# The prefetch hint in TensorE's tail names the loop's back edge instead of a stub's branch

## Chip, cores, metric

One core of one Trainium2 chip. The metric is the device time of one execution in microseconds (us). Executions agree within some 0.5 us, and a single execution of a kernel on one core is called "one run".

## The reference, cut to what matters

```python
def reference(A_x, A_k_cache, A_v_cache, A_wq, A_wo, B_x, B_w1, B_w2, B_w3, B_w4):
    # _A_ref: attention of one token over a cache of 65,536 places, 4 key/value heads
    # _B_ref: x1 = x + shifted(gelu(layernorm(x) @ w1)) @ w2;  x1 + gelu(layernorm(x1) @ w3) @ w4
    x = A_x
    xn = _layernorm(x, axis=-1)
    return x + _A_ref(xn, A_k_cache, A_v_cache, A_wq, A_wo) + _B_ref(xn, B_w1, B_w2, B_w3, B_w4)
```

Almost all of the time is the reading of the two caches (128 MiB) and of the weights: 169.87 MB in all, on a queue that keeps the sixteen DMA engines busy for 98.8% of the span.

## The kernel before

Operations are recorded per engine and emitted at the end. VectorE, ScalarE, GpSimd and SyncE run straight through; TensorE's attention part is a loop over the four heads. After the loop come the residual, the product with wo, and the product with w4, which arrives in four parts. By TensorE's sequencer is meant here what fetches its instructions. The profile shows the fetches as packets of 16,384 bytes on the queue q8, of the kind "instruction", four within the span of before. A prefetch hint is an instruction of its own (BRANCH_PREFETCH_HINT in the trace, 40 ns in before) that names a branch of the program. Around that last product the kernel before puts a stub: a hint that names a branch which is never reached (the one marked below), because the branch ahead of it always jumps over it.

```python
        def hinted_tail(eng, q, at, name):
            e = eng.engine
            one = eng.alloc_register(name + "_r")
            eng.reg_mov(one, 1)
            nc.br(name + "_b", engines=[e])
            label(name + "_b")
            hint = eng.mark_branch_hint_location()       # the hint stands here
            q.emit(eng, q.ops[at:])                      # the products with w4
            eng.br_eq(one, 1, on_true=name + "_end", on_false=name + "_t")
            label(name + "_t")
            eng.nop(nofuse=True)
            eng.br_eq(one, 0, on_true=name + "_b", on_false=name + "_end").branch_hint(hint)   # hinted, never run
            label(name + "_end")
        ...
        q_pe.emit(nc.tensor, q_pe.ops[:marks[0]])
        for s_, v in entry.items():
            nc.tensor.wait_ge(s_, v)
        with nc.tensor.Fori(0, HKV):
            for waits, o in zip(steps, work[0]):
                for s_, v in waits.items():
                    nc.tensor.wait_ge(s_, v)
                q_pe.emit(nc.tensor, [o])
            for s_, v in totals.items():
                nc.tensor.wait_ge(s_, v).then_inc(s_, -v)
        q_pe.emit(nc.tensor, q_pe.ops[marks[-1]:pe_cut])
        hinted_tail(nc.tensor, q_pe, pe_cut, "pe")
```

## Time and profile before

| | |
|---|---|
| time, median (range) | 400.37 us (400.35 to 400.45), 3 runs |
| span in the profile | 399.0 us |
| share of the data queue q1 | 98.8% of 16 DMA engines' span |
| busiest engine | VectorE, 55% |
| last landing of w4 | 396.47 us |

How to read it: here the DMA row is at 9 of 10 in 38 of its 40 slices and no engine is above 55%, so the stream of data sets the time, and the end of the kernel hangs on the last landing: 396.47 us, with 2.5 us from there to the end. The instruction queues q8 and q14 carry 0.07 and 0.02 MB, yet they use the same sixteen engines: of the sixteen landings of a load the last is 0.29 us behind the median ahead of q8's first packet, and 1.88 us on the load during which it came. The lines of the profile are in the prediction below.

### The profile page before, as it was taken

Reading aid. Unit: us, or ns where it says so; the run is one execution under the profiler, and the core shown is the slowest. Engines: PE = TensorE matmul, PEld = TensorE weight load, DVE = VectorE, ACT = ScalarE, POOL = GpSimd, SP = SyncE. Lnnn points to the kernel's source line nnn. Section 1 sums busy time; section 2 is a strip of 40 time slices with the busy share of each in tenths; the row PEclk is TensorE's granted clock in tenths of the full one; section 3 lists DMA queues with packets and bytes.
Section 4 is the critical chain, followed back from the end, with each engine's and each line's share of the span. In section 5 each row is a group of like instructions: output and inputs, shape, how many; then the busy total and the mean of one; then the engine's idle time right before and its main releaser. Section 6 shows DMA issues by size and latency. Waiting matters only on the chain.

```text
span 399.0 us, 3448 instructions
## 1 busy us (share of the span) xinstructions
PE 176.1 (44%) x1539; PEld 58.8 (15%) x1484; DVE 221.3 (55%) x260; ACT 23.9 (6%) x50; POOL 7.6 (2%) x31
## 2 busy tenths in 40 slices
PE   0034768148034713570357036413651462147394
PEld 0011334012001200120012001101120110012232
DVE  0024221995298549843984597269647952896200
ACT  1000000011001100110011002001100110011000
POOL 5000000000000000000000000000000000000000
PEclk9998656556755765565557555855585558555979
DMA  9999899999999999999999999999999999999995
GB/s 421 421 386 494 383 428 480 447 416 427 421 420 435 420 466 453 421 427 421 420 440 420 453 460 427 421 421 420 434 434 440 473 427 421 420 421 427 431 410 233
DMA packets 3759, 169.97 MB, mean 426 GB/s; under 512 B 548, under 2 KB 552, under 8 KB 808
## 3 DMA queue, kind: packets, MB, share of 16 engines
q1 hardware_dynamic: 3608, 169.87, 98.8%
q8 instruction: 4, 0.07, 0.1%
q10 hardware_dynamic: 144, 0.00, 0.0%
q14 instruction: 3, 0.02, 0.0%
HBM read 169.87 MB, written 0.00 MB: 426 GB/s over the span
## 4 chain that ended last, share of the span: by engine, by line
DMA 58%; DVE 25%; PE 13%; issue 1%; ACT 1%; SPq 1%; POOL 0%
DMA KV<-in_A_k_cache_dram 45%; DVE KV L460 18%; DMA KV<-in_B_w_dram 8%; DMA KV<-in_A_x_dram 6%; PE S_ps L411 3%; PE OT_ps L518 2%; DVE mrow L481 2%; PE M_ps L426 2%; PE S_ps L474 2%; PE S_ps L379 2%; ACT p_sb L496 1%; DVE Yall L395 1%; DVE pT_f L509 1%; PE PT_ps L505 1%; DVE pT_f L419 1%
## 5 line engine op out<-in xcount | busy, mean ns | idle before, releaser
L460 DVE STREAM_TRANSPOSE KV<-KV 128x4096 f32<-128x4096 f32 x32 | 140.3, 4421 | 43.3 <-DMA KV<-in_A_k_cache_dram 43.3
L474 PE MATMUL S_ps<-KV,Ycur 128*32 128x512 bf16 x512 | 60.7, 623 | 127.2 <-DVE KV L460 127.2
L518 PE MATMUL OT_ps<-KV,pT_f 128*32 128x512 bf16 x512 | 46.2, 500 | 1.2 <-DVE pT_f L509 1.2
L474 PEld LDWEIGHTS S_ps<-KV,Ycur 128*32 128x32 bf16 x512 | 14.3, 126 | 159.0 <-DVE KV L460 141.4
L496 ACT ACTIVATE p_sb<-S_ps,brun 128x1024 bf16<-128x1024 f32 x16 | 17.8, 1113 | 275.0 <-DVE brun L494 174.5
L509 DVE STREAM_TRANSPOSE pT_f<-PT_ps 128x512 f32<-128x512 f32 x32 | 22.5, 702 | 14.0 <-PE PT_ps L505 14.0
L481 DVE TENSOR_REDUCE mrow<-S_ps 128x1 f32<-128x1024 f32 x16 | 19.3, 1206 | 11.3 <-PE S_ps L474 11.3
L484 PE MATMUL M_ps<-Rm,Lmat 128*128 128x16 bf16 x16 | 3.1, 194 | 38.1 <-DVE Rm L482 38.1
L505 PE MATMUL PT_ps<-p_sb,permR 128*128 128x512 bf16 x32 | 18.4, 576 | 0.8
L529 DVE SCALAR_TENSOR_TENSOR O_acc<-O_acc,ff,OT_ps 128x512 f32<-128x512 f32 x12 | 9.0, 748 | 13.9 <-PE OT_ps L518 13.9
L518 PEld LDWEIGHTS OT_ps<-KV,pT_f 128*32 128x32 bf16 x512 | 12.9, 114 | 23.6 <-issue 15.5
L411 PE MATMUL S_ps<-KV 128*32 128x512 bf16 x88 | 12.6, 565 | 2.7 <-DVE KV L359 2.7
L339 DVE CAST KV<-KV 128x8 f32<-128x8 bf16 x1 | 0.2, 171 | 22.1 <-DMA KV<-in_A_x_dram 22.1
L578 PE MATMUL S_ps<-KV,o_bf 128*1 128x512 bf16 x64 | 9.4, 466 | 5.0 <-DMA KV<-in_A_wo_dram 5.0
L426 PE MATMUL M_ps<-ident_f,pT_f 64*128 64x2 f32 (+2 forms) x32 | 7.9, 372 | 2.5 <-DVE pT_f L419 2.5
L484 PEld LDWEIGHTS M_ps<-Rm,Lmat 128*128 128x128 bf16 x16 | 1.7, 104 | 49.3 <-DVE Rm L482 49.3
L582 DVE COPY pT_f<-S_ps 1x512 f32<-1x512 f32 x1 | 0.7, 679 | 14.4 <-PE S_ps L578 14.4
L426 PEld LDWEIGHTS M_ps<-ident_f,pT_f 64*128 64x128 f32 (+2 forms) x32 | 7.7, 326 | 5.0 <-DVE pT_f L419 3.4
L419 DVE COPY pT_f<-S_ps 64x512 f32<-64x512 f32 (+1 forms) x3 | 2.1, 685 | 11.3 <-PE S_ps L411 11.3
L364 PE MATMUL M_ps<-KV 8*128 8x8 bf16 x1 | 0.2, 181 | 16.0 <-DVE Dmat_f L363 16.0
L505 PEld LDWEIGHTS PT_ps<-p_sb,permR 128*128 128x128 bf16 x32 | 3.3, 103 | 26.7 <-ACT p_sb L496 14.7
L379 PE MATMUL S_ps<-KV 128*32 128x512 bf16 x64 | 6.2, 571 | 1.4 <-DVE KV L359 1.4
(88 smaller groups left out, 85.6 us busy)
## 6 DMA issues: line engine op xcount, KB each, us to landing
KV<-in_B_w_dram SPq DMA_DIRECT2D x1, 7168.0 KB, 48.2
KV<-in_B_w_dram SPq DMA_DIRECT2D x1, 4352.0 KB, 27.4
KV<-in_B_w_dram SPq DMA_DIRECT2D x2, 2048.0 KB, 28.2
KV<-in_B_w_dram SPq DMA_DIRECT2D x1, 1792.0 KB, 31.4
KV<-in_B_w_dram SPq DMA_DIRECT2D x1, 768.0 KB, 32.7
KV<-in_B_w_dram SPq DMA_DIRECT2D x1, 256.0 KB, 32.9
KV<-in_A_k_cache_dram SPq DMA_DIRECT2D x8, 46.6
KV<-in_A_v_cache_dram SPq DMA_DIRECT2D x8, 27.9
```

Source lines behind the costliest of these rows:

```text
L379: fns.append(lambda e, j=j, b=b, jj=jj: e.matmul(S_ps[32 * jj:32 * jj + 32, b, :], xn_bf[:, j:j + 1].broadcast_to([P, 32]), KV[:, 0, j * H ...
L411: fns.append(lambda e, j=j, k=k, mv=mv: e.matmul(S_ps[32 * (k % 4):32 * (k % 4) + 32, bank + k // 4, :], vec[:, j:j + 1].broadcast_to([P, ...
L426: fns.append(lambda e, b=b, nb=nb, c=c: e.matmul(M_ps[:, c0 + 16 * b + c:c0 + 16 * b + 4 * nb:4], pT_f[0:32 * nb, b, c:512:4], ident_f[0:3 ...
L460: _op(q_dve, lambda e: e.transpose(out=KV32[:, s, o:o + 4096], in_=KV32[:, s, o:o + 4096]), reads=[b_KV[s][sub]], writes=[b_KV[s][sub]], l ...
L474: fns.append(lambda e, we=we, cm=cm, mv=mv: e.matmul(S_ps[32 * cm:32 * cm + 32, n % 4, :], Ycur[:, we, :, :].rearrange("p a g -> p (a g)") ...
L481: _op(q_dve, lambda e: e.reduce_max(mrow[:, k:k + 1], S_ps[:, 2 * k:2 * k + 2, :].rearrange("p b c -> p (b c)"), axis=AX.X), reads=b_S[2 * ...
L496: _op(q_act, lambda e: e.activation(p_sb[:, :, :].rearrange("p b c -> p (b c)"), S_ps[:, 2 * k:2 * k + 2, :].rearrange("p b c -> p (b c)") ...
L505: _op(q_pe, lambda e: e.matmul(PT_ps[:, :], permR[:, :], p_sb[:, n % 2, :], start=True, stop=True), reads=[b_p[n % 2], b_const], writes=[b ...
L509: _op(q_dve, lambda e: e.transpose(out=pT_f[:, n % 2, :], in_=PT_ps[:, :]), reads=[b_PT], writes=[b_pT[n % 2]], loop=True)
L518: fns.append(lambda e, q=q, q4=q4: e.matmul(OT_ps[32 * q4:32 * q4 + 32, g % 2, :], pT_bf[:, n % 2, q, :, 1], KV[:, s, 8192 * sub + 512 * q ...
L529: _op(q_dve, lambda e: e.scalar_tensor_tensor(out=O_acc[:, 0:512], in0=O_acc[:, 0:512], scalar=ff[:, k:k + 1], in1=OT_ps[:, k, :], op0=ALU ...
L578: _grp(q_pe, [lambda e, j=j, jj=jj: e.matmul(S_ps[32 * jj:32 * jj + 1, 1, :], o_bf[:, j:j + 1], KV[:, 0, j * D + 512 * jj:j * D + 512 * (j ...
```

## The change

Its intent: the same hint with fewer instructions. It needs some branch to name; the loop's back edge exists already and is not run any more at this point, so the stub's move, its jump and its two branches can go.

```diff
-        def label(name):
-            nc.switch_bb(name, parent=None)
-
-        def hinted_tail(eng, q, at, name):
-            ... (the function shown above)
...
+        loop_br = [i for b in nc.m.functions[0].blocks for i in b.instructions if i.engine == nc.tensor.engine and "Branch" in i.opcode][-1]
         q_pe.emit(nc.tensor, q_pe.ops[marks[-1]:pe_cut])
-        hinted_tail(nc.tensor, q_pe, pe_cut, "pe")
+        bass.BassInstruction(loop_br).branch_hint(nc.tensor.mark_branch_hint_location())
+        q_pe.emit(nc.tensor, q_pe.ops[pe_cut:])
...
-        code = nc.m.functions[0].blocks[0].instructions
```

(The last line repeats an assignment made further up; without it the profile still counts 1539 matmuls and 1484 weight loads.)

## The prediction

From the recorded text (and in one place from the expectation of hint_loop_head) the passages are cut, and marked, that told of the hardware what no trace or run of this case shows, or went with that. Two figures that it uses without saying what shows them: it counts 256 instructions to a block, the piece of the program that one 16 KB packet brings. In before, TensorE had started 190, 439 and 707 instructions of the trace when the first three packets started, 249 and 268 from one to the next. And it puts some 2 us between the entry into a block and the packet of the next: in before the packets at 84.3, 120.7 and 376.8 us started 2.6, 1.7 and 2.4 us after the end of TensorE's last record ahead of them. The entry itself is not recorded, so these 2 us are an estimate, as are the 66 instructions and what is counted with them.

> **What bounds the kernel now.** I read the page of the profile first: busy shares, the row of DMA busy tenths, the DMA queues and the chain that ended last.

> ```profile
> PE 176.1 (44%) x1539; PEld 58.8 (15%) x1484; DVE 221.3 (55%) x260; ACT 23.9 (6%) x50; POOL 7.6 (2%) x31
> ...
> DMA  9999899999999999999999999999999999999995
> ...
> q1 hardware_dynamic: 3608, 169.87, 98.8%
> q8 instruction: 4, 0.07, 0.1%
> ...
> q14 instruction: 3, 0.02, 0.0%
> ...
> DMA 58%; DVE 25%; PE 13%; issue 1%; ACT 1%; SPq 1%; POOL 0%
> ```

> No engine is busy for more than 55% of the span, while the data queue q1 keeps the sixteen DMA engines busy for 98.8% of it: the kernel is one long stream of 169.87 MB. The change can matter in two ways only: by TensorE instructions in the tail, or by the traffic that fetches instructions (q8, four packets of 16 KB in 0.07 MB; q14, three of 8 KB), which shares those DMA engines. So I read next the chain of waits in the last 36 us and the timeline of TensorE from 389 us on (start, length, what).

> ```profile
> 363.55 32.92 DMA KV<-in_B_w_dram
> 396.47 0.04 issue
> 396.51 0.31 PE S_ps L566 x4
> 396.82 0.02 issue
> 396.85 0.42 DVE orow L648
> ```

> ```profile
> 390.24 0.61 PE L584 MATMUL S_ps<-pT_f,ident_f 64*1 64x256 f32 x8 [1.40 <-ACT pT_f L583]
> 390.77 2.03 PE L566 MATMUL S_ps<-KV,gh_bf 128*1 128x256 bf16 x68
> 394.00 0.93 PE L566 MATMUL S_ps<-KV,gh_bf 128*1 128x256 bf16 x28 [1.20 <-DMA KV<-in_B_w_dram]
> 395.86 0.50 PE L566 MATMUL S_ps<-KV,gh_bf 128*1 128x256 bf16 x12 [0.92 <-DMA KV<-in_B_w_dram]
> 396.51 0.28 PE L566 MATMUL S_ps<-KV,gh_bf 128*1 128x256 bf16 x4 [0.16 <-DMA KV<-in_B_w_dram]
> ```

> The last weight load, w4, comes in four parts (17, 7, 3 and 1 rows). TensorE finishes the 68 products of the first part at 392.80 and then stands still for 1.20, 0.92 and 0.16 us for the next three. The end is set by the landing of the last part at 396.47; behind it are only four matmuls, one copy of 0.42 us and the output DMA. Last, the pages of the lines of the stub:

> ```profile
> L670 PEldq MOVE  x1: 29/29/29, 390.3 to 390.3; - x1
> ...
> L673 PEldq BRANCH_PREFETCH_HINT  x1: 40/40/40, 390.3 to 390.3; - x1
> ...
> L675 PEldq COMPARE_BRANCH  x1: 246/246/246, 396.5 to 396.5; - x1
> ...
> L713 PEldq COMPARE_BRANCH  x4: 87/225/237, 140.8 to 373.0; - x4
> ```

> They give min/median/max in ns and the first and last start in us. The stub costs a move of 29 ns and a hint of 40 ns ahead of the w4 products, and a taken branch of 246 ns behind the last of them. The loop's own back edge costs 223 to 237 ns when taken and 87 ns the last time.

> [...] q8's packets are 16,384 bytes each, starting at 48.1, 84.3, 120.7 and 376.8 us. [...] a loop trip is 556 weight loads and matmuls (278 of each, from the counts of lines 474, 518, 505, 484, 543 and 535 over 4), more than two blocks, yet after the first trip (65.6 to 140.8 us) nothing is fetched on q8 until the loop is over. The loop stays resident. [...]

> [...] The trace has these sixteen landings for each load. With respect to the median engine the last of them is 0.29 us late at 26 us, but 1.88 us late on the load during which the fetch of 48.1 us came; then a second engine is 0.79 us late (the 8 KB fetch at 55.0), and the fetches at 84.3, 120.7 and 376.8 each make one more engine late. For w4's last part five engines are late by 1.18, 1.43, 1.57, 1.58 and 1.62 us. So one 16 KB fetch delays its engine by 1.2 to 1.7 us, and the load waits for the latest engine, not for the sum.

> [...] The trace has 87 ns not taken and 223 to 246 ns taken[...].

> **The change part by part.** The instruction order of the two kernels is the same on VectorE, ScalarE, GpSimd and SyncE. On TensorE:

> Removed ahead of the w4 products: the move, 29 ns; the unconditional branch to the next block left no record in the trace, so 0. The first w4 products could start up to 0.03 us earlier. They are followed by 1.20 us of waiting for a DMA: 0 on the path.

> Removed behind the last product: the branch of 246 ns at 396.52, done at 396.76, and an instruction and a second branch that were never run. VectorE's copy ends at 397.27 and the output's landing is waited for until 399.0, so TensorE was not last: 0 on the path.

> Kept: the hint, 40 ns, at the same place. Its branch is now the loop's back edge, behind it, with the loop's head as target. That is the open part. The built program of TensorE has 1,380 entries before and 1,374 after, labels included. The four q8 packets fit block boundaries if some 66 instructions precede the kernel's own (an estimate from where TensorE was at these times). Then the next boundary, 1,280, falls at entry 1,214: inside the first w4 group, after the hint at entry 1,151. A sequential prefetch should have followed there, about 391 us, with its packet some 2 us later. The trace has none. So I take it that the armed hint made the sequencer look at the hinted target instead, which is in a block already held. In the changed kernel the target is the head of the loop, also held (four trips without a fetch). I expect again no fetch.

> Moved: the loop's label on every engine is now the target of a hinted branch and is marked for alignment in the built program, where before it was the stub's label. With the estimate of 66 the head lies at 444, 68 short of a boundary; I don't expect it to move.

> Sum: 0 - 0 + 0 = 0.0 us, with at most 0.1 us from noise in where packets fall.

> **The rivals.** First: the hint of a branch that lies behind holds nothing back, and the block after the tail is fetched at about 391 us, 16 KB. For it: the absence of that packet before needs a cause, and the stub's branch lay ahead, in the very block being entered. Against its costing much: so far every fetch of TensorE made a new engine late, and a new engine has room: late by up to 1.2 us when w4's last landing is already 1.62 us behind the median. Cost 0; but if it falls on one of the five late engines (5 of 16, if the choice were free), 1.2 to 1.6 us, so 401.6 to 402.0.

> Second: the sequencer fetches the loop's head or shifts the blocks because of the alignment. The landing of a fetched block costs the same as above; a stall of TensorE would need over 1.20 us in the w4 group before it shows, or 396.5 us as its moment. A miss there of some 3 us (the 1.0 us packet and about 2 us ahead of it, my estimate) would leave 1.8 us: 402.2.

> Third: it gets faster, because a fetch that now delays w4 goes away. One candidate is the fetch at 376.8; but the code up to the hint is the same, entry for entry, and removing it would leave the other four late engines. Gain 0. The same holds for the 8 KB packet at 393.65, whose engine is only 0.43 us late.

> **The range and the chances.** No fetch, 80%: 400.3 to 400.5. A hidden fetch, 11%: the same. A fetch on a late engine, a moved loop or a stall, 7%: 401.5 to 402.5. Something that I don't see, 2%. The runs before lie between 400.35 and 400.45. I predict 400.4 us, 400.1 to 400.9 for eight in ten. Two per cent are 8 us, which nothing above reaches: within 2% 0.985, slower 0.01, faster 0.005.

> **What would show it.** Right: four q8 packets at the same times; w4's parts landing at 379.3, 389.6, 394.0, 395.8 and 396.5 us (wo's among them, first); the wait of 1.20 us ahead of the 28 products within 0.05 us; no compare-and-branch after the last matmul; a back edge of 223 to 237 ns as before. Wrong in the first step: a fifth q8 packet after 390 us, and a sixth late engine. Wrong in the second: a q8 packet inside the loop's later trips, or a gap inside the 68 products, which now issue in groups of four every 0.1 us. A time under 400.1 would mean that some landing came earlier, thus that a fetch left the late engines, for which I see no cause.

## The result and the profile after

The changed kernel takes 400.41 us (median of 6 runs, 400.31 to 400.60), the kernel before in the same rounds 400.42 us (6 runs, 400.35 to 400.58). The ratio is 1.0, 95% interval 0.9987 to 1.0013. A ratio here is the mean time of one kernel's fast runs over the mean of the other's of the same rounds, so not quite the ratio of the medians.

The page of the changed kernel, the DMA row and the queues:

```profile
DMA  9999999999999999999999999999999999999995
...
q1 hardware_dynamic: 3608, 169.87, 98.7%
q8 instruction: 5, 0.08, 0.1%
...
q14 instruction: 3, 0.02, 0.0%
```

There is one packet more on q8 than before, five in place of four. The chain of waits at the end, and TensorE's timeline from 389 us on:

```profile
363.63 32.91 DMA KV<-in_B_w_dram
396.54 0.04 issue
396.58 0.31 PE S_ps L566 x4
396.89 0.02 issue
396.92 0.42 DVE orow L648
```

```profile
389.67 0.61 PE L584 MATMUL S_ps<-pT_f,ident_f 64*1 64x256 f32 x8 [1.39 <-ACT pT_f L583]
390.21 2.03 PE L566 MATMUL S_ps<-KV,gh_bf 128*1 128x256 bf16 x68
394.07 0.93 PE L566 MATMUL S_ps<-KV,gh_bf 128*1 128x256 bf16 x28 [1.84 <-DMA KV<-in_B_w_dram]
395.93 0.50 PE L566 MATMUL S_ps<-KV,gh_bf 128*1 128x256 bf16 x12 [0.92 <-DMA KV<-in_B_w_dram]
396.58 0.28 PE L566 MATMUL S_ps<-KV,gh_bf 128*1 128x256 bf16 x4 [0.16 <-DMA KV<-in_B_w_dram]
```

The last load takes 32.91 us against 32.92; the waits ahead of the last two groups are the same to 0.01 us. TensorE reached w4 0.56 us earlier (390.21 against 390.77) and only waited longer for it, 1.84 us in place of 1.20. That head start isn't the stub's 0.03 us: the 64 products with wo took 8.76 us here against 9.39. Nor is it the change's: looked at once more, the kernel before took 8.76 us for them and the changed kernel 9.26 (again_before, again_after). The pages of the hint and of the loop's control lines:

```profile
L704 PEldq BRANCH_PREFETCH_HINT  x1: 50/50/50, 389.7 to 389.7; - x1
...
L695 PEldq COMPARE_BRANCH  x4: 76/219/252, 140.6 to 374.0; - x4
```

No compare-and-branch is left behind the last product.

The page does not say when a packet came; the trace records it. In this table are the starts, in us, of all 16 KB packets of q8 within the span; further the latest of the sixteen landings of w4's last part, how far it lies behind the median of the sixteen, and how many engines are over 1 us behind it. An engine counts as late whatever made it so, also by the 8 KB packets of q14, of which more below the last experiment. The experiments told of below stand in the table too.

| kernel (profiled run) | 16 KB instruction packets at | last landing | behind the median | late engines | span |
|---|---|---|---|---|---|
| before | 48.1, 84.3, 120.7, 376.8 | 396.47 | 1.62 | 5 | 399.0 |
| again_before | 48.1, 84.8, 123.0, 378.2 | 396.90 | 2.06 | 5 | 399.4 |
| after | 48.0, 84.2, **200.2**, 378.5, **394.0** | 396.54 | 1.56 | 6 | 399.1 |
| again_after | 48.0, 84.1, **200.2**, 378.2, **394.1** | 396.93 | 2.10 | 5 | 399.4 |
| no_hint | 48.1, 84.1, 123.1, 377.1, **394.2** | 396.42 | 1.64 | 5 | 398.9 |
| hint_loop_end | 48.1, 84.0, 120.4, 378.5, **393.6** | 396.38 | 1.48 | 6 | 398.9 |
| hint_ahead_loop | 47.9, 84.2, **197.9**, 378.6, **393.8** | 396.50 | 1.48 | 6 | 399.0 |
| loop_then_stub | 45.9, 84.5, 120.6, 378.3 | 396.49 | 1.58 | 5 | 399.0 |
| early_reset | 46.0, 84.3, 120.3, 378.6, **393.7** | 396.80 | 1.86 | 6 | 399.4 |
| stub_early | 46.1, 84.3, 120.6, 378.4 | 396.50 | 1.53 | 5 | 399.1 |
| stub_late | 45.8, 84.1, 120.6, 378.3 | 396.80 | 1.88 | 5 | 399.3 |
| hint_loop_head | 46.1, 82.0, **378.3, 384.9, 394.3** | 396.51 | 1.61 | 5 | 399.0 |
| one_block_more | **14.2**, 47.7, 86.5, 122.9, 378.2 | 396.62 | 1.73 | 6 | 399.1 |

(Bold: what differs from the kernel before.) So the time is as predicted, but the fetches are not: the third moved from 120.7 to 200.2 us, into the loop's second trip, and a fifth came at 394.0, in the tail.

### The profile page after: what moved, and what is told of

It reads as the page before. It is cut to its first block, busy times and chain, and to the rows that moved or that the text cites. A ratio compares the mean times of both kernels' runs of the same rounds, so it can differ in the third digit from the quotient of the medians.

```text
span 399.1 us, 3446 instructions
## 1 busy us (share of the span) xinstructions
PE 177.2 (44%) x1539; PEld 59.9 (15%) x1484; DVE 221.3 (55%) x260; ACT 23.9 (6%) x50; POOL 7.6 (2%) x31
## 3 DMA queue, kind: packets, MB, share of 16 engines
q1 hardware_dynamic: 3608, 169.87, 98.7%
HBM read 169.87 MB, written 0.00 MB: 426 GB/s over the span
## 4 chain that ended last, share of the span: by engine, by line
DMA 58%; DVE 25%; PE 13%; issue 1%; ACT 1%; SPq 1%; POOL 0%
DMA KV<-in_A_k_cache_dram 45%; DVE KV L460 18%; DMA KV<-in_B_w_dram 8%; DMA KV<-in_A_x_dram 6%; PE S_ps L411 3%; PE OT_ps L518 2%; DVE mrow L481 2%; PE M_ps L426 2%; PE S_ps L474 2%; PE S_ps L379 2%; ACT p_sb L496 1%; DVE Yall L395 1%; DVE pT_f L509 1%; PE PT_ps L505 1%; DVE pT_f L419 1%
## 6 DMA issues: line engine op xcount, KB each, us to landing
KV<-in_B_w_dram SPq DMA_DIRECT2D x1, 7168.0 KB, 48.1
```

## The experiments

Rivals: B, the loop's label, which the hint marks for alignment, moved the code; C, the fifth packet is made by the hint itself, which names a branch behind it; D, the moments vary by themselves; E, a hint holds back the next prefetch whichever block is entered. All eleven kernels gave a correct result.

**again_before** and **again_after**: both kernels once more, unchanged.

> The kernel before, unchanged, profiled once more. Theory A (a hint stays armed until its branch is passed, and when TensorE enters the block that holds the hinted branch, the hinted target is fetched in place of the next block; the target is already held, so nothing is fetched): again four 16 KB packets of instructions, near 48, 84, 121 and 377 us, and none after 390. Rival D (the moments vary from execution to execution): the third packet somewhere else, or a fifth one. Time 400.4 by both.

> The changed kernel, unchanged, profiled once more. Theory A: five packets, near 48, 84, 200, 378 and 394 us: the hint left armed at the end of one execution diverts the fetch of the first loop trip in the next one, so the third packet waits for the second trip. Rival D: the third packet at 121 or the fifth missing. Time 400.4, ratio within 0.1% of before, because the fifth packet goes to an engine that has room.

Measured: the packets of each kernel are where they were, within 2.3 us (table); the two that moved moved again. Rival D is out. again_after: 400.43 us (5 runs, 400.40 to 400.70), before in the same rounds 400.43 (9 runs, 400.19 to 400.73), ratio 1.0, interval 0.9987 to 1.0014. again_before was one run, 400.65 us: that is the noise that one look has.

**no_hint**: the changed kernel without the hint.

```diff
-        bass.BassInstruction(loop_br).branch_hint(nc.tensor.mark_branch_hint_location())
```

> The changed kernel without any hint. Theory A: nothing is armed, so the plain sequence: packets near 48, 84, 121, 377 and 394 us, five in all. Rival C (the hint of a branch that lies behind itself makes the fetch of 394 us, of the loop's head): four packets, none after 390. Rival B (the loop's label, marked for alignment through the hint, moved the blocks): as theory A here, third packet at 121. Time: 400.4 as long as the fifth packet finds an engine with room; 401.6 to 402.0 if it falls on a late one.

Measured: 48.1, 84.1, 123.1, 377.1, 394.2. The queues on its page:

```profile
q8 instruction: 5, 0.08, 0.1%
q14 instruction: 2, 0.02, 0.0%
```

The fifth packet comes without any hint, at 394.2 us, so it is the plain fetch of the next block, and rival C is out: the stub's hint takes it away (none after 376.8 us in before), the back edge's hint doesn't (394.0 in after). The third is back at 123. Time 400.36 us (5 runs, 400.18 to 400.61), ratio to before 1.0, interval 0.9986 to 1.0014: neither hint is worth any time. Not foreseen: q14 has two packets of 8 KB here, not three; the one that comes between 392.8 and 394.3 us in all twelve profiles with a hint does not come within this trace. A hint also marks a label of the program for alignment, which might be the cause; that is argued only, and no run here separates it.

**hint_loop_end**: the hint of the back edge at the end of each trip, just ahead of its branch.

```diff
             for s_, v in totals.items():
                 nc.tensor.wait_ge(s_, v).then_inc(s_, -v)
+            at_end = nc.tensor.mark_branch_hint_location()
...
+        bass.BassInstruction(loop_br).branch_hint(at_end)
-        bass.BassInstruction(loop_br).branch_hint(nc.tensor.mark_branch_hint_location())
```

> The hint of the loop's back edge moved from the tail to the end of each loop trip, just ahead of that branch; the loop's label is marked for alignment as in the changed kernel. Theory A: the hint is used up by its own branch a few instructions on, without a block being entered in between, so the sequence is plain: packets near 48, 84, 121, 377 and 394 us. Rival B (alignment): the third packet at 200 us as in the changed kernel. Time 400.4 by both; the back edge may become shorter than its 220 to 250 ns, hidden.

Measured: 48.1, 84.0, 120.4, 378.5, 393.6; one run, 400.14 us. The label carries the same mark as in the changed kernel, and the third packet is back in the first trip: rival B is out. The back edge did not become shorter: 223 to 242 ns when taken.

**hint_ahead_loop**: the same hint once, ahead of the loop.

```diff
+        ahead = nc.tensor.mark_branch_hint_location()
         with nc.tensor.Fori(0, HKV):
...
+        bass.BassInstruction(loop_br).branch_hint(ahead)
-        bass.BassInstruction(loop_br).branch_hint(nc.tensor.mark_branch_hint_location())
```

> The hint of the loop's back edge stands once, ahead of the loop, and none in the tail. Theory A: the first trip enters the block of the back edge with the hint armed, so the third packet moves from 121 to 200 us; the tail has no hint, so the fifth stays at 394: 48, 84, 200, 378, 394. If the 200 us of the changed kernel did not come from a hint armed in the first trip, the third packet is at 121 here. Time 400.4.

Measured: third packet at 197.9, a fifth at 393.8; one run, 400.37 us. A hint armed in the first trip is enough to move the third fetch into the second trip.

**loop_then_stub**: the kernel before with the back edge's hint put ahead of its stub.

```diff
         q_pe.emit(nc.tensor, q_pe.ops[marks[-1]:pe_cut])
+        bass.BassInstruction(loop_br).branch_hint(nc.tensor.mark_branch_hint_location())
         hinted_tail(nc.tensor, q_pe, pe_cut, "pe")
```

> Both hints in the tail, first that of the loop's back edge, then that of the stub. Theory A with one place for an armed hint: the second replaces the first, so as the kernel before: 48, 84, 121, 377, none after 390. With a place for each hint: 48, 84, 200, 378 and none after 390. Time 400.4 by both.

Measured: third at 120.6, no fifth; one run, 400.26 us. The second hint replaced the first: by these two moments there is one place.

**early_reset**: the stub's hint at the very start of TensorE's code, the back edge's in the tail.

```diff
+        hint = nc.tensor.mark_branch_hint_location()
         q_pe.emit(nc.tensor, q_pe.ops[:marks[0]])
...
         q_pe.emit(nc.tensor, q_pe.ops[marks[-1]:pe_cut])
+        bass.BassInstruction(loop_br).branch_hint(nc.tensor.mark_branch_hint_location())
         hinted_tail(nc.tensor, q_pe, pe_cut, "pe")
...
-            hint = eng.mark_branch_hint_location()
```

> The stub's hint at the very start of TensorE's code, and the loop's hint in the tail as in the changed kernel. If the changed kernel's third packet at 200 us comes from a hint left armed by the execution before, and there is one place for it, the early hint replaces it: third packet back at 121; in the tail the loop's hint replaces the stub's, so a fifth packet at 394. If nothing is carried over and the hint of the tail did it in another way, third packet at 200. With a place for each hint: 200, and none at 394. Time 400.4.

Measured: third at 120.3, a fifth at 393.7; one run, 400.68 us. The tail is that of the changed kernel as far as the hint goes, and a hint at the start, which by theory A overwrites what was left, puts the third fetch back. So the hint of one execution does reach into the next. One loophole: the stub's code is in this tail too, and its taken branch might have dropped the hint; no run has that code with the back edge's hint alone. The next two runs speak against it, for there a hint outlives taken branches.

**stub_early**: the kernel before with its hint moved to the very start.

```diff
+        hint = nc.tensor.mark_branch_hint_location()
         q_pe.emit(nc.tensor, q_pe.ops[:marks[0]])
...
-            hint = eng.mark_branch_hint_location()
```

> The kernel before with its hint moved from the tail to the very start of TensorE's code. Theory A: the hint waits for the block of its branch, the last one: 48, 84, 121, 377, none after 390, as before. Rival E (a hint only holds back the next prefetch, whichever block is entered): the packet at 48 is missing, TensorE stalls near 84 us for the block, and there is one at 394. Time 400.4 by theory A.

Measured: all four, none in the tail; one run, 400.37 us. The hint waited for 390 us, through three taken back edges of the loop, for the block of its own branch. Rival E is out.

**stub_late**: the kernel before with its hint behind the first 68 products of w4.

```diff
-            q.emit(eng, q.ops[at:])
+            n1 = next(i for i in range(at + 1, len(q.ops)) if q.ops[i][0] == 0 and i > at + 40)
+            q.emit(eng, q.ops[at:n1])
+            hint = eng.mark_branch_hint_location()
+            q.emit(eng, q.ops[n1:])
```

> The kernel before with the stub's hint behind the first 68 products of w4, so behind the entry into the last block at some 391 us. Theory A: on the first execution the fetch is already asked for; but the hint stays armed over the end, because its branch is never run, so later executions enter the block with it armed: 48, 84, 121, 377 and none after 390. If nothing is carried from one execution to the next: a fifth packet at 394. Time 400.4.

Measured: the hint ran at 392.8 us, and there is no fifth packet; one run, 400.56 us. This points the same way as early_reset, and here the hint outlived the stub's own taken branch at 396.9 us. That a hint so soon after the entry still stopped a fetch already asked for is not ruled out by this run alone.

**hint_loop_head**: the hint at the head of each trip, none in the tail.

```diff
         with nc.tensor.Fori(0, HKV):
+            at_head = nc.tensor.mark_branch_hint_location()
...
+        bass.BassInstruction(loop_br).branch_hint(at_head)
-        bass.BassInstruction(loop_br).branch_hint(nc.tensor.mark_branch_hint_location())
```

> The hint of the loop's back edge at the head of each trip[...], none in the tail. Theory A: every trip enters the block of the back edge with the hint armed, so the next block is never fetched in the loop; after the loop TensorE runs into it unprepared near 374 us: no packet at 121, one at about 375 on demand, and a stall of 2 to 4 us among the 32 small products of line 572, ahead of the wait for wo at 379.4 us, which hides it: time 400.4. If the stall runs beyond 379.4 us it comes out of the 1.2 us of slack ahead of the 28 products of w4. Rival B: no stall, packets as in the changed kernel.

Measured: no packet between 82.0 and 378.3 us. TensorE's timeline behind the loop:

```profile
373.91 0.50 PE L572 MATMUL S_ps<-ident_f,acc 128*1 128x64 f32 x10
380.72 1.23 PE L572 MATMUL S_ps<-ident_f,acc 128*1 128x64 f32 x20 [6.31 <-issue]
381.74 9.12 PE L578 MATMUL S_ps<-KV,o_bf 128*1 128x512 bf16 x64
...
392.79 2.79 PE L566 MATMUL S_ps<-KV,gh_bf 128*1 128x256 bf16 x96
395.91 0.93 PE L566 MATMUL S_ps<-KV,gh_bf 128*1 128x256 bf16 x16 [0.32 <-DMA KV<-in_B_w_dram]
```

"issue" is time in which the engine waited for nothing that the profile shows: 6.31 us in the middle of one group, around the packet of 378.3. It is the stall that theory A foresaw, well over the 2 to 4 us that I had guessed (an estimate, around the prediction's 3 us: 1.0 us for the packet and about 2 us ahead of it). It goes 1.3 us beyond 379.4, the landing of wo, and TensorE comes to w4 2.0 us later than in the kernel before (392.79 against 390.77). Of the three waits for w4 the first is gone (96 products run through), the second has shrunk from 0.92 to 0.32 us, and the third still stands: 0.15 us, inside the last line, which merges 12 and 4 products. Time 400.43 us (4 runs), before 400.48 (9 runs), ratio 0.9998, interval 0.9982 to 1.0013: even a stall of 6.31 us cost nothing here.

**one_block_more**: the kernel before with a block of useless instructions early on.

```diff
+        _grp(q_pe, [lambda e, k=k: e.matmul(M_ps[0:8, 480:488], (ident_bf[0:8, 0:8], selGT_bf[0:8, 0:8])[k % 2], ident_bf[0:8, 0:8], start=True, stop=True)
+                    for k in range(128)], reads=[b_const], writes=[b_M], partial=True)
```

> The kernel before with 128 small, useless matmuls early on, while TensorE is idle: 256 instructions, one block more, all later blocks shifted by exactly one. Theory of the late engines (the load waits for the latest engine, a 16 KB packet makes one engine late by 1.2 to 1.8 us, each on another one): five packets, the fifth between 5 and 15 us, one more late engine, time 400.4, within 0.1%. If packets cost by their sum, 16 KB of 170 MB is 0.04 us, not to be told apart; if it falls on an engine that is late already, 1.2 us or more: 401.6.

Measured: the extra work, in its place,

```profile
6.82 3.34 PE L362 MATMUL M_ps<-KV 8*8 8x8 bf16 x128
```

and five packets, the first at 14.2 us. Six engines are now over 1 us behind the median in place of five, the last by 1.73 us. Time 400.40 us (5 runs, 400.30 to 400.47), before 400.48 (9 runs), ratio 0.9997, interval 0.9983 to 1.0010. One more whole block costs nothing that could be measured. The time alone would also fit a price by bytes (0.04 us, as the expectation says); that the block went to an engine of its own is seen in the landings, not in the time.

What decides the time of a single run shows in the table: the span less the last landing is 2.5 to 2.6 us in all thirteen profiles, and the last landing follows from how far the latest engine is behind: 1.48 us with a span of 398.9 at the one end, 2.10 us with 399.4 at the other. The number of packets, four or five, does not order the spans.

What the longer spans have in common comes from two packets that no experiment was about, the 8 KB ones of q14 near 55 and 259 us. In before, the landings of the load that ends at 243.8 us have one engine 0.78 us behind the median and three over 1.5; at 263.2 us, after the second of these packets, none is near 0.78 any more and four are over 1.5, the latest 1.74. So both packets fell on one engine, and on one engine the delays add up; this is the fifth late engine beside the four of the 16 KB packets. The same step, by 0.95 to 0.98 us, is in all thirteen profiles. After it the latest engine is 1.61 to 1.82 us behind in the nine with spans of 398.9 to 399.1 us and 2.05 to 2.21 in the four of 399.3 and 399.4. That is read from the landings, which name no engine; no run changed these packets, so it is a fit and not a test.

## Why the prediction was right, and where it was not

- **The time**: right, 400.4 predicted, 400.41 measured, a change of nothing. The main line, no fetch at 80%, did not happen; what happened is the hidden fetch, given 11%, and it was the pricing of this rival that made the number right.
- **Removed ahead of w4, 0.03 us, off the path**: right. The wait ahead of the 28 products took in much more than that, 0.56 us in after and 2.0 us the other way in hint_loop_head. Its own check, that wait within 0.05 us of 1.20, failed: it was 1.84 us, through the faster group of wo. The check was too narrow, for the kernel before itself has 1.83 us in again_before.
- **Removed behind the last product, 246 ns, off the path**: right; it is gone, and 2.5 us still lie between last landing and end.
- **Kept: "I expect again no fetch"**: wrong, and this is the step that failed. From the missing packet I had concluded that an armed hint makes the sequencer look at the hinted target, whichever block is entered. The next block's fetch is held back only when the block of the hinted branch is entered (stub_early: the hint ran at the very start, all four packets came, and none in the tail; hint_ahead_loop: the packets at 47.9 and 84.2 us came, the third only at 197.9). Both signs that the prediction had set for this, a fifth packet after 390 us and a sixth late engine, came. Its first rival, given at most 18%, had the right ground for it: the stub's branch lay "in the very block being entered". A hint of a branch two blocks back, by the estimate of the blocks, lets the fetch through (394.0 us in after).
- **The rival's price**: right, 0. The fifth packet made a sixth engine late, by 1.08 us in after, and that engine stayed ahead of the latest, 1.56 us. So the wrong step cost nothing in the sum. The packet is also so late that its engine may have done its share: those that started at 393.6 to 394.0 us made a sixth engine late, those at 394.1 to 394.3 (again_after, no_hint, hint_loop_head) did not. The reason given, "late by up to 1.2 us", was weaker than it looked: the prediction's own line has 1.2 to 1.7 us, and 1.88 right after a fetch, which is over the 1.62 of the latest engine. It also put the five late engines down to 16 KB packets, of which there were four; the fifth engine is q14's, by the fit above. None of the seven fetches in the tail raised the latest engine, but what picks the engine stays open, so that part is luck as far as these runs show.
- **The loop untouched**: wrong in one point that I had not thought of. The third fetch moved to the second trip, because the hint outlived the execution (early_reset). That is the sign set for the second rival, a packet in a later trip, but not its cause, alignment (hint_loop_end). Harmless: the block is needed only after the loop (in hint_loop_head, with no packet between 82.0 and 378.3 us, TensorE stood still from 374.4 us on, behind the last trip). The stall that this rival priced at some 3 us was 6.31 us where it did come (hint_loop_head), 0 on the time there; its sum with this size, 400.4 + 6.31 - 1.20, would be 405.5 in place of 402.2 (an estimate).
- **Moved labels**: right for TensorE, the packets of hint_loop_end are those of before and one more. For q14 open.

What stays open: what a hint does when its target is not held (in all runs here it was taken to be), on which engine a block's fetch falls, and what a 16 KB fetch on the latest engine would cost, which no run had.

## What to carry to other kernels

Where the DMA stream bounds a kernel as it does here (98.8% of the span), price an instruction fetch by the engine that it delays, not by its bytes: TensorE took up the last part of w4 0.04 us after the latest of its sixteen landings, which was 1.62 us behind the median (before), and a fetch on an engine with room cost nothing that could be measured (one_block_more: ratio 0.9997, interval 0.9983 to 1.0010). In these kernels a prefetch hint acted at the block of the branch that it names, so it could not be pointed at just any branch: the stub's took the fetch at 394 us away, the back edge's moved the third from 120.7 to 200.2 us. If it is to hold back a fetch, name a branch in the block where that fetch is asked for, and remember that an unused hint was still armed in the next execution (third packet at 200.2 us in after, at 120.3 in early_reset). And an effect that can be seen in the trace (a packet that is gone or moved) is not yet a gain: look first at how long the engine waits afterwards for something else.

Other figures of TensorE in before and after: a hint ran 40 and 50 ns, a compare-and-branch 208 to 252 ns when taken and 87 and 76 ns when not. A loop trip of 556 weight loads and matmuls ran three more times without a fetch in before. Running straight on into a block that had not come cost a stall of 6.31 us, with the DMA row at 9 of 10 (hint_loop_head).
